# A gated delta rule in chunks of 64 on 64x64 TensorE tiles, its blocks inverted on VectorE, in front of a Fourier mixing block

## The chip, the core and the metric

The kernel runs on one core of a Trainium2 chip. TensorE multiplies matrices, VectorE, ScalarE and GpSimd work on elements, SyncE (SP) issues most transfers. The metric is the device time of one execution in microseconds; lower is better.

## What is computed

Four batches, eight heads, 768 tokens of 48 channels. Per head a 48x48 state is read by the query and corrected by each token; the heads' outputs, side by side (384 channels), go through a Fourier mixing over tokens and channels, a normalization and a two-layer channel mix.

```python
for t in range(S):
    y[:, :, t] = np.einsum('bhd,bhde->bhe', q[:, :, t], state)
    v_old = np.einsum('bhde,bhd->bhe', state, kt)
    state = state + bt[:, :, :, None] * np.einsum('bhd,bhe->bhde', kt, vt - v_old)
...
X = np.fft.fft(np.fft.fft(x, axis=1), axis=2)
u = x + np.real(X)
un = (u - mu) / np.sqrt(var + 1e-06)
out = u + np.maximum(un @ w_ch1, 0.0) @ w_ch2
```

All matrix work is in float32; the two weights arrive as 64-bit floats and are turned into float32 on VectorE, with a last multiplication on GpSimd.

## The kernel before, in words

The attention goes through each batch in six chunks of 128 tokens, 24 chunks in all, each with all eight heads. `load` fetches K, V and q of a chunk. `pre(n)` normalizes K (a power on GpSimd, L304), transposes keys and queries on TensorE (`pt`, L321), forms the Gram products (`pg`, L337) and from them `AT`, `LQ` and the block-diagonal `Abd`. Within a chunk, tokens depend on earlier ones through a triangular matrix. `pre` inverts its 32x32 diagonal blocks in five levels (loop at L361): `px` multiplies a widened block-diagonal matrix by the inverse so far, VectorE masks it into `Y`, `widen` (L353) spreads `Y` and the transposed inverse over 128 columns on VectorE and GpSimd, and `pn` multiplies again. Each of these matmuls has a 128x128 weight and 32 moving columns, one for each head.

`seq(n)` is the chain over chunks: `pk` (keys times state, L410), `R`, then four times over a 32-row strip `pu` (L425), a copy `U` on ScalarE, `pa` (L420) and a subtraction; then `pS` (the state's update, L433), `py` (the output, L437 and L439), and the state's add on VectorE (L443).

`post(b)` does all that follows for a batch: sums and differences on VectorE and the matmuls `pf`, `pb`, `pd` of the Fourier stage, their adds into `x` (L512), statistics, and in three groups of 256 tokens the transposes `ptr`, the first layer `ph` (L566, 36 matmuls of 256 columns), relu on ScalarE and VectorE in turn, the second layer `po` (L577, 24 matmuls of 384 columns), and the stores.

`weights()` converts the six 1.5 MB pieces of the two weights. All of these are generators. The loop at L599 takes a piece of `seq(n)`, a piece of `pre(n + 1)` and a piece of `side` in turn; `side` is `weights()` during batch 0 and `post(b - 1)` after. `post` of the last batch stands alone behind the loop. The framework's scheduler then fixes each engine's order from these pieces; every engine works in order. A float32 matmul shows as two records in the trace, a weight load (PEld) and a matmul (PE) for each.

Of the kernel before, what the change touches and what calls it, by code (L numbers as in the profile page):

```python
# [16 lines left out]
C = 128  # L17
W = 32
LEVELS = (1, 2, 4, 8, 16)


def _consts(B, S, DM):

    p = np.arange(128)
    c = np.arange(W)
    r = p % W
    ident = np.eye(128)
    su = (p[None, :] > p[:, None]).astype(np.float64)
    bd = su * (p[None, :] // W == p[:, None] // W)
    grp = (p[:, None] // W == np.arange(128 // W)[None, :]).astype(np.float64)  # L30
    eye_c = (r[:, None] == c[None, :]).astype(np.float64)
    lev = []
    for n in LEVELS:
        off = ((r[:, None] // n) % 2 == 1) & (c[None, :] // n == r[:, None] // n - 1)
        lev.append(eye_c - off)
    pack = np.concatenate([ident, su, bd, grp, eye_c] + lev, axis=1)
# [45 lines left out]
def kernel(  # L82
# [23 lines left out]
    HV = (5 * H + 7) // 8  # L106
# [4 lines left out]
    io = ctx.enter_context(tc.tile_pool(name="io", bufs=2))  # L111
# [3 lines left out]
    def ps_pre(shape, name):  # L115
        return ps.tile(shape, F32, tag="pre", bufs=3, name=name)

    def ps_seq(shape, name):
        return ps.tile(shape, F32, tag="seq", bufs=2, name=name)

    def ps_post(shape, name):
        return ps.tile(shape, F32, tag="post", bufs=3, name=name)
# [9 lines left out]
    NKQ = 2  # L132
    kqs = []
    for i in range(NKQ):
        t = const.tile([128, 3, H, 64], F32, name=f"kq{i}")
        nc.gpsimd.memset(t, 0.0)
        kqs.append(t)
    states = []
    for i in range(2):
        t = const.tile([128, NP, 2, D], F32, name=f"state{i}")  # L140
        nc.gpsimd.memset(t, 0.0)
        states.append(t)

    steps = [(b, c) for b in range(B) for c in range(NC)]
    loaded = {}

    def load(n):
        b, c = steps[n]
        kq = kqs[n % NKQ]
        K4 = io.tile([128, H, D], F32, tag="K4", name="K4")  # L150
        V4 = io.tile([128, H, D], F32, tag="V4", name="V4")

        first = c * C + (1 if c < TH else 0)
        m = C - 1 if c == TH - 1 else C
        cuts = (0, 112, m) if m < C else (0, m)
        for dst, src in ((K4, k), (kq[:, 2, :, 0:D], q), (V4, v)):
            for i, j in zip(cuts, cuts[1:]):
                nc.sync.dma_start(out=dst[i:j],
                                  in_=src[b, :, first + i:first + j, :].rearrange("h p d -> p h d"))
            if m < C and src is q:  # L160
                nc.sync.dma_start(out=dst[m:C],
                                  in_=cn["zrow"].ap().rearrange("p (h d) -> p h d", h=H))
            elif m < C:
                nc.sync.dma_start(out=dst[m:C],
                                  in_=src[b, :, 0:1, :].rearrange("h p d -> p h d"))
        loaded[n] = (K4, V4)

    pack = const.tile([128, 3 * 128 + NG + W * (1 + len(LEVELS))], F32, name="pack")
    nc.scalar.dma_start(out=pack, in_=cn["pack"].ap())
    bt = const.tile([NBH, S], F32, name="bt")  # L170
    bflat = beta.rearrange("b h s -> (b h) s")
    nc.gpsimd.memset(bt[:, S // 2 - 1:S // 2], 0.0)
    nc.scalar.dma_start(out=bt[:, 0:S // 2 - 1], in_=bflat[:, 1:S // 2])
    nc.scalar.dma_start(out=bt[:, S // 2:S], in_=bflat[:, S // 2:S])
    load(0)
# [10 lines left out]
    m_su = pack[:, 128:256]  # L186
    m_bd = pack[:, 256:384]
    o = 3 * 128
    m_grp = pack[:, o:o + NG]
    eye_c = pack[:, o + NG:o + NG + W]  # L190
    m_lev = [pack[:, o + NG + W * (i + 1):o + NG + W * (i + 2)] for i in range(len(LEVELS))]

# [455 lines left out]
```

## Time and profile before

| | |
|---|---|
| median of 3 runs | 1946.74 us (1942.17 to 1961.88) |
| profiled execution | 1932.67 us |
| its span, first to last instruction | 1930.9 us |
| TensorE matmuls busy | 1843.2 us, 95% |
| TensorE weight loads busy | 1626.1 us, 84% |
| VectorE busy | 629.6 us, 33% |
| GpSimd busy | 449.5 us, 23% |
| ScalarE busy | 244.1 us, 13% |
| mean granted clock of TensorE | 0.895 |

How to read it: busy time is the time in which an engine has an instruction in work, so 95% says that something is nearly always in TensorE, not that its array is full. [...] Durations of single matmul records overlap, since they are pipelined; what a group costs is read from the time that it takes as a whole.

### The profile page before, as it was taken

How to read it: one execution, taken by the hardware profiler on the slowest of the kernel's cores; microseconds unless marked ns; L12 is line 12 of the kernel's file. 1: busy time of each engine (PE TensorE's matmuls, PEld its weight loads, DVE VectorE, ACT ScalarE, POOL GpSimd, SP SyncE). 2: the span in 40 equal slices, each digit the busy share in tenths (PEclk: the TensorE clock that was granted, in tenths of full speed). 3: DMA queues.
4: the chain of work that ended last, by engine and by line, in shares of the span. 5: the costliest groups of instructions: out<-in, count | busy, mean ns of one | idle time of the engine just before them, and what ended most of it. 6: DMA issues, size and time to landing. Idle time of an engine off the chain costs nothing. (4 is left out here: it accounts for less than half of the span.)

```text
span 1930.9 us, 26464 instructions
## 1 busy us (share of the span) xinstructions
PE 1843.2 (95%) x11782; PEld 1626.1 (84%) x11782; DVE 629.6 (33%) x1142; ACT 244.1 (13%) x481; POOL 449.5 (23%) x381
## 2 busy tenths in 40 slices
PE   5899898989999999999999999999999999999898
PEld 5898898989898897988888987888798888888576
DVE  4333433433323321323242332323323333222410
ACT  0101011010111101111101011101110111111110
POOL 3331312222221221313220322233211232122100
PEclk9999999999999857879975599999955699899899
DMA  5101101000000000001000000000000000000000
GB/s 145 38 9 41 37 5 45 9 5 13 5 5 5 13 9 9 13 13 21 9 13 5 9 14 18 9 14 21 13 9 1 13 9 9 1 9 2 9 8 17
DMA packets 80710, 31.47 MB, mean 16 GB/s; under 512 B 76116, under 2 KB 77716, under 8 KB 80212
## 3 DMA queue, kind: packets, MB, share of 16 engines
q1 hardware_dynamic: 78964, 25.96, 5.7%
q0 software_dynamic: 768, 2.36, 0.3%
q8 instruction: 92, 1.51, 0.3%
q10 hardware_dynamic: 864, 1.47, 0.2%
q14 instruction: 22, 0.18, 0.0%
HBM read 25.06 MB, written 4.72 MB: 15 GB/s over the span
## 5 line engine op out<-in xcount | busy, mean ns | idle before, releaser
L125 PEld LDWEIGHTS pn<-Tn,Yx 128*128 128x128 f32 x1536 | 259.9, 260 | 23.9 <-issue 18.1
L125 PE MATMUL pn<-Tn,Yx 128*128 128x32 f32 x1536 | 255.5, 331 | 16.5 <-DVE Yx L356 15.2
L125 PE MATMUL ph<-unT,w 128*128 128x256 f32 x864 | 248.8, 431 | 1.9 <-ACT unT L560 1.9
L356 POOL TENSOR_TENSOR TTx<-Tn,pack 128x384 f32<-128x384 f32 x96 | 133.6, 1392 | 482.0 <-ACT Tn L385 385.9
L356 POOL TENSOR_TENSOR Yx<-Y,pack 128x384 f32<-128x384 f32 x120 | 146.3, 1220 | 392.7 <-DVE Y L368 321.3
L125 PEld LDWEIGHTS px<-Tn,Abd 128*128 128x128 f32 x1152 | 197.0, 264 | 29.1 <-ACT Tn L385 25.2
L125 PE MATMUL px<-Tn,Abd 128*128 128x32 f32 x1152 | 200.0, 339 | 16.8 <-ACT Tn L385 16.8
L125 PEld LDWEIGHTS pn<-Y,TTx 128*128 128x128 f32 x1152 | 196.2, 262 | 19.2 <-DVE Y L368 15.2
L125 PE MATMUL po<-w,hT 128*128 128x384 f32 x576 | 209.9, 503 | 0.0
L125 PE MATMUL pn<-Y,TTx 128*128 128x32 f32 x1152 | 195.8, 335 | 10.8 <-DVE Y L368 10.8
L356 DVE TENSOR_TENSOR TTx<-Tn,pack 128x640 f32<-128x640 f32 x96 | 83.4, 869 | 374.5 <-ACT Tn L385 313.6
L125 PEld LDWEIGHTS ph<-unT,w 128*128 128x128 f32 x864 | 172.0, 213 | 27.8 <-ACT unT L560 2.8
L125 PEld LDWEIGHTS po<-w,hT 128*128 128x128 f32 x576 | 104.6, 193 | 56.6 <-issue 0.6
L125 PE MATMUL pg<-KQT,K1T 48*128 48x128 f32 x768 | 143.6, 369 | 2.7 <-ACT KQT L323 2.7
L125 PEld LDWEIGHTS pg<-KQT,K1T 48*128 48x128 f32 x768 | 117.7, 254 | 15.7 <-ACT KQT L323 4.4
L368 DVE TENSOR_TENSOR Y<-px,pack 128x256 f32<-128x256 f32 x120 | 50.8, 424 | 242.1 <-PE px L125 242.1
L356 DVE TENSOR_TENSOR Yx<-Y,pack 128x640 f32<-128x640 f32 x120 | 126.5, 1054 | 5.7 <-DVE Y L368 0.5
L125 PEld LDWEIGHTS pu<-R,Tn 32*32 32x32 f32 x1536 | 94.3, 130 | 33.1 <-issue 16.3
L385 ACT ACTIVATE Tn<-pn 128x512 f32<-128x512 f32 x72 | 43.0, 597 | 593.6 <-PE pn L125 569.0
L421 DVE TENSOR_TENSOR R<-R,pa 32x384 f32<-32x384 f32 x72 | 39.8, 553 | 218.1 <-PE pa L125 217.9
L125 PE MATMUL pu<-R,Tn 32*32 32x48 f32 x1536 | 109.6, 236 | 0.7
L125 PEld LDWEIGHTS pa<-U,AT 64*32 64x32 f32 (+2 forms) x1152 | 71.9, 134 | 21.0 <-issue 15.0
(107 smaller groups left out, 1826.3 us busy)
## 6 DMA issues: line engine op xcount, KB each, us to landing
w<-in_moe_w_ch_dram SPq DMA_DIRECT2D x6, 1536.0 KB
K<-in_k_dram SPq DMA_DIRECT2D x20, 192.0 KB
V<-in_v_dram SPq DMA_DIRECT2D x20, 192.0 KB
kq<-in_q_dram SPq DMA_DIRECT2D x20, 192.0 KB
out_dram<-x SPq DMA_DIRECT2D x8, 192.0 KB
kq<-in_q_dram SPq DMA_DIRECT2D x4, 168.0 KB
K<-in_k_dram SPq DMA_DIRECT2D x4, 168.0 KB
V<-in_v_dram SPq DMA_DIRECT2D x4, 168.0 KB
```

The lines of the kernel that those rows point to most:

```text
L125: nc.tensor.matmul(o, lhsT=lhsT, rhs=rhs, start=start, stop=stop, skip_group_check=True)
L356: eng.tensor_tensor(t[:, hs], src[:, hs, None, :].broadcast_to(shape), m_grp[:, None, :, None].broadcast_to(shape), op=ALU.mult)
L368: nc.vector.tensor_tensor(Y, px, m_lev[i][:, None, :].broadcast_to([128, H, W]), op=ALU.mult)
L385: nc.scalar.activation(Tn, pn, ACT.Copy)
L421: nc.vector.tensor_tensor(R[rw], R[rw], pa[rw], op=ALU.subtract)
```

## The change

The attention is written anew; `post`, `weights` and the stores keep their arithmetic.

- Chunks have 64 tokens, 48 in all. Four heads lie side by side in the lower half of the partitions and four in the upper half (`hh`), and four chunks make a quad, of which there are 12. A quad's K, q and V come in 24 loads.
- `prepare(Q)` does for a quad what `pre` did up to the Gram products. `pg` is a matmul of 48 rows by 64 columns; the four combinations of row half (`e`) and column half (`hh`) follow each other.
- `invert(g)` takes two quads: eight chunks of eight heads with two blocks of 32x32 each, 128 blocks, one for each partition. Four 32x32 block transposes on VectorE bring each block onto one partition (`X`, 32x32 elements), 30 steps of a multiplication and an addition with broadcasts invert all of them, and six transposes bring them back. Four rounds of 32 small matmuls (`pj`, 32x32x32) join the two blocks of a chunk, and GpSimd scales the result `wt` by beta.
- `chain(m)` has no strips: `pk`, `R`, one `pu`, `U`, `pS` with the state's add (two state tiles in turn), `py`.
- The loop takes six pieces of `pre` (now `prepare` and `invert` of the group ahead) and eight of `side` for each chunk. The first group is prepared and inverted wholly before the first chunk.
- In PSUM, buffers are two pairs of banks, two single ones and two for `post` (three before). The weight staging and `hT` have one buffer (two before), K and q one.

```diff
-C = 128
+CH = 64
...
+    def invert(g):
+        A = grams.pop(g)
+        wt = wts[g % 2]
+        X = wk.tile([128, W, W], F32, tag="X", name="X")
+        for i in range(4):
+            pr, c0 = slice(32 * i, 32 * i + 32), W * (i % 2)
+            nc.vector.transpose(X[pr], A[pr, :, :, c0:c0 + W].rearrange("p c u s -> p s (c u)"))
+        yield
+        for j in range(1, W - 1):
+            n = W - 1 - j
+            t = wk.tile([128, 240], F32, tag="sub", bufs=2, name="sub")
+            t = t[:, 0:n * j].rearrange("p (k i) -> p k i", k=j)
+            nc.vector.tensor_tensor(t, X[:, j:j + 1, j + 1:].broadcast_to([128, j, n]),
+                                    X[:, 0:j, j:j + 1].broadcast_to([128, j, n]), op=ALU.mult)
+            nc.vector.tensor_tensor(X[:, 0:j, j + 1:], X[:, 0:j, j + 1:], t, op=ALU.add)
+            if j % 2 == 0:
+                yield
...
+        for lh in range(2):
+            js = wk.tile([128, QT, 4, W], F32, tag="js", name="js")
+            for step in range(2):
...
+                            if step == 0:
+                                ops = A[r2, n, u, 0:W], wt[r2, n, u, W:]
+                            else:
+                                ops = T1[r1, n, u], js[r1, c, u]
+                            mm(pj[r1, hh, c, u], *ops, c == 0 and u == 0)
...
+            nc.gpsimd.tensor_tensor(w, w, bb[:, :, :, None].broadcast_to([128, QT, 4, CH]), op=ALU.mult)
...
-        for j in range(NP):
-            mm(pk[:, 2 * j:2 * j + 2, :], KQT[:, 0, j, :], st[:, j], j == 0)
+        for j in range(2):
+            for hh, e in ((0, 0), (1, 1), (0, 1), (1, 0)):
+                pr = slice(64 * e, 64 * e + D)
+                mm(pk[64 * hh:64 * hh + 64, e, j], KQT[pr, c, j, hh, 0, :], st[pr, hh, j, e, :], j == 0)
...
-        for g in range(NG):
...
-                for h in range(H):
-                    mm(pa[rw, h, :], AT[0:W * g, h, rw], U[0:W * g, h, :], h == 0)
...
+        for u in range(4):
+            for hh in range(2):
+                pr = slice(64 * hh, 64 * hh + 64)
+                mm(pu[pr, u], wt[pr, at, u], R[pr, u], u == 0)
...
+    run(ahead(0))
+    tables()
+    side, pre = weights(), iter(())
+    for m in range(STEPS):
...
+        live = True
+        step = chain(m)
+        shares = [6, 8]
+        while live or any(shares):
+            live = live and advance(step)
+            for i, gen in enumerate((pre, side)):
+                for _ in range(2):
+                    if shares[i]:
+                        shares[i] -= 1
+                        advance(gen)
+    run(side)
+    run(post(B - 1))
```

TensorE before, at a chunk of batch 2 that runs beside the first layer of `post(1)` (`ident` and `eye` start each level's product, `x3` means three in a row):

```order
L125 MATMUL ph<-unT,w_98 128x256 x2
L125 LDWEIGHTS ident_b
L125 MATMUL px<-eye_b,ident_b 128x256
L125 MATMUL px<-Y,Abd 128x32 x8
L125 MATMUL ph<-unT,w_98 128x256 x3
L125 MATMUL pn<-Y,TTx 128x32 x8
L125 MATMUL ph<-unT,w_98 128x256 x3
L125 MATMUL pn<-Tn,Yx 128x32 x8
```

TensorE in the change, a chunk of batch 1 beside the first layer of `post(0)`:

```order
L124 MATMUL pk<-st_76,KQT 64x48 x8
L127 MATMUL ptr<-pack,un 128x128 x6
L124 MATMUL pu<-R,wt_74 64x48 x8
L124 MATMUL ph<-unT,w_125 128x256 x18
L124 MATMUL pS<-U,kp_64 48x48 x8
L124 MATMUL py<-st_76,KQT 64x96 x4
L124 MATMUL py<-U,LQ 64x48 x8
L124 MATMUL ph<-unT,w_125 128x256 x12
```

Where the inverse's matmuls stood between pieces of `ph`, the chain's own groups of eight stand now, and a whole chunk passes within some thirty `ph`.

VectorE in the change, between the last chunk of batch 1 and the first of batch 2: the end of `invert` (`X`, `wt`, `T`) and of the Fourier stage of `post(1)` (`x<-x,pb`), then `R` of the chunk:

```order
L377 TENSOR_TENSOR sub<-X 128x30
L554 TENSOR_TENSOR x<-x,pb 128x193
L379 TENSOR_TENSOR X<-X,sub 128x30
L585 BN_AGGR mv<-bst 128x2
L554 TENSOR_TENSOR x<-x,pb 128x191
L386 STREAM_TRANSPOSE wt_74<-X 32x32x32
L389 STREAM_TRANSPOSE T_3656<-X 32x32x32
...
L597 TENSOR_SCALAR un<-x,mv,rstd 128x384 x3
L452 TENSOR_TENSOR R<-V_3247,pk 128x2x2x48
```

TensorE at the same place:

```order
L124 MATMUL pb<-dtab,F 128x191 x2
L124 MATMUL pd<-dtab,gz 32x193 x2
L124 MATMUL pj<-wt_74,A 32x32 x32
L124 MATMUL pj<-js,T_3656 32x32 x32
L124 MATMUL pj<-wt_74,A 32x32 x32
L127 MATMUL ptr<-pack,un 128x128 x6
L124 MATMUL pj<-js,T_3656 32x32 x32
L124 MATMUL pk<-st_76,KQT 64x48 x8
```

Here the inverse of the next group, the whole Fourier stage and the four rounds of `pj` stand in front of the first chunk of the batch on both engines.

## Rows read from the trace of the kernel before

**Rows 1.** Page: busy times, granted clock in 40 slices, transfer rate by slice.
```profile
PE 1843.2 (95%) x11782; PEld 1626.1 (84%) x11782; DVE 629.6 (33%) x1142; ACT 244.1 (13%) x481; POOL 449.5 (23%) x381
...
PEclk9999999999999857879975599999955699899899
...
GB/s 145 38 9 41 37 5 45 9 5 13 5 5 5 13 9 9 13 13 21 9 13 5 9 14 18 9 14 21 13 9 1 13 9 9 1 9 2 9 8 17
```

**Rows 2.** Groups of TensorE by form: busy us, mean ns; idle before, releaser.
```profile
L125 PE MATMUL pn<-Tn,Yx 128*128 128x32 f32 x1536 | 255.5, 331 | 16.5 <-DVE Yx L356 15.2 <-DVE nrm L306 1.2
L125 PE MATMUL ph<-unT,w 128*128 128x256 f32 x864 | 248.8, 431 | 1.9 <-ACT unT L560 1.9
L125 PE MATMUL po<-w,hT 128*128 128x384 f32 x576 | 209.9, 503 | 0.0
L125 PE MATMUL px<-Tn,Abd 128*128 128x32 f32 x1152 | 200.0, 339 | 16.8 <-ACT Tn L385 16.8
L125 PE MATMUL pn<-Y,TTx 128*128 128x32 f32 x1152 | 195.8, 335 | 10.8 <-DVE Y L368 10.8
```

**Rows 3.** Timeline, 100 to 118 us: start, duration, engine, instructions, idle before.
```profile
103.51 3.46 PE L125 MATMUL px<-pack,Abd 128*128 128x32 f32 x16
106.90 1.48 PE L125 MATMUL pu<-R,Tn 32*32 32x48 f32 x16
...
108.42 0.48 ACT L426 ACTIVATE U<-pu 32x384 f32<-32x384 f32 x1 [7.61 <-PE pu L125]
...
108.95 1.09 PE L125 MATMUL pS<-U,kq 128*64 128x48 f32 x16 [0.57 <-ACT U L426]
```

**Rows 4.** Timeline, two places at the higher clock, 1152 and 1195 us.
```profile
1152.14 1.03 PE L125 MATMUL pk<-state,KQT 128*128 128x96 f32 x8
...
1153.00 1.91 PE L125 MATMUL px<-Tn,Abd 128*128 128x32 f32 x16
...
1195.66 2.85 PE L125 MATMUL po<-w,hT 128*128 128x384 f32 x8
...
1198.44 0.67 PE L125 MATMUL pS<-U,kq 128*64 128x48 f32 x16
```

**Rows 5.** By stage: length, busy of PE, PEld, DVE, ACT, POOL; clock; DMA.
```profile
640.00:1114.00 474.00, 469.01 (x3046) 411.50 (x3044) 147.13 (x271) 61.84 (x122) 115.37 (x100) 0.75 0.05 12
1114.00:1404.00 290.00, 289.44 (x2343) 246.25 (x2342) 96.48 (x165) 47.18 (x95) 79.91 (x64) 0.98 0.07 15
1404.00:1527.00 123.00, 119.69 (x608) 111.08 (x607) 40.91 (x88) 13.47 (x25) 25.13 (x26) 0.50 0.04 7
...
1800.00:1931.00 131.00, 115.33 (x472) 84.19 (x471) 31.50 (x86) 13.59 (x31) 8.81 (x12) 0.96 0.03 11
```

**Rows 6.** Timeline, the first load of K and its first use.
```profile
0.72 0.45 SPq L158 DMA_DIRECT2D K<-in_k_dram  x1
...
4.59 0.82 POOL L301 TENSOR_TENSOR Ksq<-K 128x384 f32<-128x384 f32 x1
```

**Rows 7.** Groups of VectorE by form.
```profile
L339 DVE TENSOR_TENSOR Abd<-pg,pack 128x512 f32<-128x512 f32 x48 | 33.2, 691 | 66.2 <-PE pg L125 66.1
...
L512 DVE TENSOR_TENSOR x<-x,pb 128x191 f32<-128x191 f32 x72 | 20.9, 346 | 0.0
...
L412 DVE TENSOR_TENSOR R<-Vb,pk 128x384 f32<-128x384 f32 x24 | 13.1, 545 | 11.4 <-PE pk L125 11.4
...
L267 DVE TENSOR_SCALAR wtmp<-w 128x768 int32<-128x768 int32 x12 | 7.2, 601 | 6.7 <-POOL w L286 6.6
```

**Rows 8.** Groups of ScalarE and GpSimd by form.
```profile
L382 ACT ACTIVATE Tn<-pn 128x256 f32<-128x256 f32 x48 | 18.4, 384 | 262.5 <-PE pn L125 246.2 <-DVE wtmp L271 9.8 <-POOL nrm L304 6.6
...
L304 POOL TENSOR_TENSOR nrm<-nrm,half_p 128x8 f32<-128x8 f32 x24 | 41.6, 1732 | 22.6 <-DVE nrm L303 22.6
...
L286 POOL TENSOR_TENSOR w<-wtmp 128x768 f32<-128x768 f32 x12 | 24.0, 2000 | 30.4 <-DVE wtmp L285 28.8 <-DVE nrm L305 1.6
...
L546 POOL TENSOR_TENSOR rstd<-rstd,half_n 128x2 f32<-128x2 f32 x12 | 8.7, 728 | 1.0
```

More of the change, by code (lines that the diff above doesn't have):

```diff
@@ L15 @@
 ACT = mybir.ActivationFunctionType
-C = 128
+CH = 64
 W = 32
-LEVELS = (1, 2, 4, 8, 16)
+QT = 4
 def _consts(B, S, DM):
     p = np.arange(128)
[L25 to L36, printed above, removed]
+    t = np.arange(CH)
+    before = (t[None, :] > p[:, None] % CH).astype(np.float64)
+    lower = -(t[None, :] < p[:, None] % CH).astype(np.float64)
+    pack = np.concatenate([np.eye(128), before, lower], axis=1)
     half = S // 2
@@ L129, in tr @@
                          is_transpose=True, start=start, stop=True, skip_group_check=True)
[L132 to L144, printed above, removed]
-    loaded = {}
@@ L147, in load @@
[L147 to L166, printed above, removed]
@@ L168, with zeroed @@
-    pack = const.tile([128, 3 * 128 + NG + W * (1 + len(LEVELS))], F32, name="pack")
+    def zeroed(shape, name, eng):
+        t = const.tile(shape, F32, name=name)
+        eng.memset(t, 0.0)
+        return t
+    kps = [zeroed([128, QT, 4, 64], f"kp{i}", nc.gpsimd if i else nc.vector) for i in range(NB)]
+    qps = [zeroed([128, QT, 4, 64], f"qp{i}", nc.vector) for i in range(1)]
+    wts = [zeroed([128, 2 * QT, 4, CH], f"wt{i}", nc.gpsimd) for i in range(2)]
+    sts = [zeroed([128, 2, 2, 2, D], f"st{i}", nc.gpsimd) for i in range(2)]
@@ L352, in widen @@
-        def widen(src, tag):
-            t = wk.tile([128, H, NG, W], F32, tag=tag, name=tag)
-            for eng, hs in ((nc.vector, slice(0, HV)), (nc.gpsimd, slice(HV, H))):
-                shape = [128, hs.stop - hs.start, NG, W]
-                eng.tensor_tensor(t[:, hs], src[:, hs, None, :].broadcast_to(shape),
-                                  m_grp[:, None, :, None].broadcast_to(shape), op=ALU.mult)
-            return t.rearrange("p h g w -> p h (g w)")
-        T = TT = TTx = None
@@ L444, in seq @@
-        nc.scalar.activation(xs[b][:, c if c < TH else NC + TH - 1 - c, :], py.rearrange("p h d -> p (h d)"), ACT.Copy)
+        last = n == NCH - 1
+        pk = ps_pair("pk")[:, :, 0:2 * D].rearrange("p e (j d) -> p e j d", j=2)
+        for j in range(2):
+            for hh, e in ((0, 0), (1, 1), (0, 1), (1, 0)):
+                pr = slice(64 * e, 64 * e + D)
+                mm(pk[64 * hh:64 * hh + 64, e, j], KQT[pr, c, j, hh, 0, :], st[pr, hh, j, e, :], j == 0)
+        R = wk.tile([128, 4, D], F32, tag="R", bufs=2, name="R")
@@ new lines, in chain @@
+        if not last:
+            pS = ps_pair("pS")[:, :, 0:2 * D].rearrange("p h (j d) -> p h j d", j=2)
+            for j in range(2):
+                for hh, e in ((0, 0), (1, 1), (0, 1), (1, 0)):
+                    pr = slice(64 * hh, 64 * hh + 64)
+                    mm(pS[64 * e:64 * e + D, hh, j], kp[pr, c, 2 * j + e, 0:D], U[pr, 2 * j + e], j == 0)
+            for e in range(2):
+                pr = slice(64 * e, 64 * e + D)
+                nc.vector.tensor_tensor(nst[pr, :, :, e, :], st[pr, :, :, e, :], pS[pr], op=ALU.add)
```

396 lines of the change are left out of this document (212 added, 184 removed).

## The prediction

> **What bounds the kernel now.** I read the page's busy times first. TensorE's matmuls fill 95% of the span, VectorE, GpSimd and ScalarE a third or less [rows 1]: this is a TensorE kernel. Then the groups of its instructions, shapes apart: three groups of the triangle inverse (`pn`, `px`; 128-column weights, 32 moving columns) take 651 us, the two products of the channel mix (`ph`, `po`) 459 us [rows 2]. Third, the clock. [...] In the rows by stage the granted clock is 0.50 in 1404 to 1527, where TensorE is as busy as elsewhere, but with short attention matmuls and the Fourier stage, 0.98 in 1114 to 1404, where `ph` and `po` run beside them, and 0.96 at the end, where the post stage runs alone [rows 5]. So attention is not only the larger half of the work, it also holds the clock down where nothing else runs.
>
> **What goes, what comes.** The inverse by levels goes: `pn`, `px` (the 651 us and their smaller groups), the widening `Yx`, `TTx` on VectorE and GpSimd, and the serial `pu`, `pa` ladder of 32-row strips. The post stage stays instruction for instruction. What comes, by prices:
>
> *TensorE.* Attention now works in 64x64 tiles. The nearest row is `pS`, already 64 columns wide and on two column halves in turn: sixteen records (eight matmuls) in 0.67 us at full clock [rows 4], 1.09 at half [rows 3]. I take that for each of `pk`, `pu`, `pS` and the `LQ` part of `py`. Below it: half, if four tiles run at once. Above it: 1.91, the 128-column price [rows 4]. The state part of `py` (four matmuls, 96 columns) I put at 0.6, between half of `pk`'s 1.03 [rows 4] and all of it. One chunk: 4 x 0.67 + 0.6 = 3.3 us. Per eight chunks `prepare` and `invert` add 32 transposes (0.12 each from 1.91 / 16, 3.8 us), 64 `pg` matmuls of 128 columns in two tiles (0.12, 7.7) and 128 `pj` matmuls of 32 columns (0.06, 7.7): 2.4 per chunk. Changing tile shape costs about 0.1: `px` starts 0.17 before the modelled end of `pk`, same shape, `pS` 0.07 before that of `po` [rows 4]. Eight changes a chunk: 0.8. Together 6.5 us per chunk, 48 chunks, 312 us, where attention now takes some 1,300 of 1843 (`ph`, `po` and the small Fourier groups taken off).
>
> *The chain.* A chunk is `pk`, `R` on VectorE, `pu`, `U` on ScalarE, `pS`, and `py` before the next `pk`; the state's add (0.35 twice) lies beside `py`. With TensorE otherwise empty, so at the lower clock: 3 x 1.09 + 0.35 + 0.38 + (1.09 + 1.3) + about 0.4 of hand-offs (0.05 from `U`'s end at 108.90 to `pS` [rows 3]) = 6.8 us. 192 elements on VectorE cost 0.35 [rows 7].
>
> *VectorE.* Two rows give a price, 0.346 for 191 elements and 0.545 for 384 [rows 7]: 0.15 us and 1.03 ns an element. `invert`'s sixty multiply and add instructions hold 9,920 elements in all: 9 + 10.2 = 19 us per eight chunks. No row shows STREAM_TRANSPOSE. Ten of them with 1,024 elements: by the same price 1.2 each, which I take, 12 us (floor 0.35 each, 4; ceiling double, 24). Two `prepare` add 10.8 (reduction and scaling of 768 elements 0.94 each, `A` and `LQ` 0.69 each four times [rows 7], small ones 0.6). Together 42 us per eight chunks. GpSimd's power on 16 columns: 0.73 for 2, 1.73 for 8 [rows 8], so 3.1.
>
> *Costed at nothing.* ScalarE's new copies (48 `U` at 0.38, 48 `x`, 48 to 72 transposed chunks, 48 `pj`, by 0.38 for 256 elements [rows 8]) and GpSimd's masks stay under a third of the span and run beside TensorE. SP now issues 24 loads a quad in place of 6 for the same tokens; at 0.45 [rows 6] that is 11 us in the 60 and more that a quad will take. The q loads wait for the last chunk transposes of the quad before, K's for its scaling, and a weight piece and the next V wait behind them in SP's queue. Their cover is the rest of the quad; without it a quad's `prepare` starts some 11 us late, 12 times, and half of that, 65 us, is in the range.
>
> **The sum by stages, along the new order.**
> 1. *Before the first `pu`* nothing hides the set-up. K comes in eight issues of 0.45 instead of one that let the square start at 4.59 [rows 6]: 7.7; square 2, reduction 0.9, power 3.1, rest 1.7: 15.4. Chunk transposes and Gram products at half clock: 28. Second quad: 46. Then the inverse: transposes 5, the sixty 19, thirty weight instructions between them 14 (0.45; 0.60 for 768 elements [rows 7]), transposes out 7: 91. The four `pj` rounds are serial (matmuls 1.9, two copies 0.6 each, hand-offs): 14; GpSimd's scaling of `wt`, twice 1,024 elements at 2.0 per 768 [rows 8]: 5. **110 us.**
> 2. *Batch 0, twelve chunks.* VectorE sets it: weights, 11 parts of ten instructions, 50; `pre` of the next group 42, half of the one after 11; chain 13; the second `pj` and scaling, 19; and seven chunks with little on VectorE, where the chain is 3 us longer each: 22. **157 us.** The single weight buffer adds a load behind each piece; the order puts transposes and small rows ahead of the next use, about 10 us. At the 145 GB/s of the page's first slice [rows 1] a load of 1.57 MB is 11 us, so uncovered loads would cost up to 5 x 11 = 55: that goes into the range.
> 3. *Batches 1 to 3.* Post alone now takes 126 of the last 131 us with TensorE busy 115 [rows 5]. To its 126 add the attention's 12 x 6.5 = 78; the inverse's tail of 19 us one and a half times a batch, half of it beside `ph`, 14; three chunks after post has run out, 10; the Fourier stage at the lower clock, 10; less the 16 us that TensorE idles in the window, which attention fills. 222 each, **666 us.** Relu copies lie behind at most eight small rows (2.5 us) on VectorE; two `ph` matmul groups in front of them cover 2.6.
> 4. *Post of batch 3*, as now: **131 us.**
>
> 110 + 157 + 666 + 131 = 1064. The profiled execution is 1932.67 for a span of 1930.9, and the median of the runs stands 0.7% above it: (1064 + 2) x 1.007 = **1075 us.**
>
> **Rivals.** (a) *Post does not keep the clock up.* A matmul burst is now followed by chain waits. [...] For it: 0.75 over 640 to 1114, although TensorE was never idle there [rows 5]. Against: `ph` and `po` will be over half of TensorE's time, more than in the stretch at 0.98. Chance 0.12. [...]
> (b) *Tiles take turns.* If 64x64 tiles in different rows don't overlap as the column halves of `pS` do, a group of eight costs 1.1 in place of 0.67 (16 records at half the 128-column spacing, and the tail): about 3.4 more per chunk on 36 chunks, 35 in the first stages: 1230 us. Chance 0.1.
> (c) *Small VectorE rows are dear.* `invert`'s pairs depend on each other; at 0.67 instead of 0.32 each, 360 rows add 126, and they stand ahead of `R`: 1200 us. Chance 0.1.
> (d) *Better than priced.* Four tiles at once, transposes at their floor, loads all covered: 36 x 2 + 50 less, some 950. Chance 0.12.
> (e) *Slower than before.* The same place as (c): 870 us over 360 rows needs 2.4 us more for each, seven times the nearest row. Chance 0.02.
> My forecast keeps 0.54 with 990 to 1170 as its own range.
>
> **Range and chances.** From below (d)'s middle to most of (a): 960 to 1300. Faster by over 1% 0.97, within 1% (about what a measurement of this kernel can tell from no change) 0.01, slower 0.02; every case but (e) ends far below.
>
> **What would show it.** The first `pu` near 110 us; twelve `py` of batch 0 done by about 270; `pk` of batch 2 after a gap of some 50 us, behind `X` rows and Fourier rows on VectorE; groups of eight 64-column matmuls at 0.67 us; the clock at 1.0 under `ph` and `po` and 0.5 in set-up and batch 0; post alone at the end for 131 us. TensorE busy should fall from 95% to some 65%. Wrong would be a first `pu` after 150, `pS` over 1 us at full clock, a low clock under `ph`, or STREAM_TRANSPOSE over 2.4 us.

## The result, and the profile after

The changed kernel takes 1004.83 us (median of 4 runs, 999.34 to 1005.39); the kernel before took 1944.61 us on the same chip. The ratio is 0.515 (95% interval 0.512 to 0.518). The forecast was 1075, with a range of 960 to 1300. The profiled execution is 1004.53 us, its span 1002.8.

First the page: the busy row of TensorE with the others, and the granted clock in forty slices. Columns of the busy row: us, share of the span, instructions.

```profile
PE 748.7 (75%) x7768; PEld 566.9 (57%) x7768; DVE 547.6 (55%) x1200; ACT 150.5 (15%) x337; POOL 172.4 (17%) x136
...
PEclk9555556555586989997557999999879999879999
```

TensorE's 95% of [rows 1] is 75% of half the time, and VectorE's share went from a third to 55%. The clock digits stand at 5 to 6 until a quarter of the span is over, and at 7 to 9 for nearly all of the rest; the two 5s in the middle are the gap ahead of batch 2 (below). The 9 of the first slice is not what the rows there show: two `pt` records take 0.63 us at 19.11, as they do at 478.62, in that gap, where the granted clock is 0.50.

The span in the stages of the prediction: set-up (to the first `pk`), batch 0 (to the end of its last `py`), batches 1 to 3 with the post stage of the batch before, the last post. Columns: stretch, length, busy time of TensorE matmuls, weight loads, VectorE, ScalarE and GpSimd (instructions), granted clock, DMA share, GB/s.

```profile
0.00:118.00 118.00, 29.70 (x480) 23.83 (x480) 78.33 (x155) 11.02 (x21) 43.33 (x33) 0.62 0.30 70
118.00:267.40 149.40, 82.87 (x1342) 70.66 (x1341) 119.74 (x253) 21.41 (x47) 40.54 (x26) 0.53 0.23 61
267.40:478.20 210.80, 179.60 (x1805) 134.27 (x1804) 113.64 (x248) 34.91 (x80) 34.20 (x26) 0.86 0.12 24
478.20:692.30 214.10, 184.55 (x2060) 137.24 (x2060) 122.89 (x268) 39.34 (x88) 34.86 (x27) 0.87 0.11 23
692.30:870.20 177.90, 159.34 (x1640) 118.01 (x1638) 81.64 (x195) 29.99 (x70) 11.95 (x13) 0.94 0.05 12
870.20:1002.80 132.60, 112.62 (x456) 82.87 (x454) 31.37 (x85) 13.79 (x31) 7.52 (x11) 0.93 0.03 9
```

| stage | forecast | measured |
|---|---|---|
| up to the first `pu` | 110 | 121.0 (the first `pk` stands at 118) |
| batch 0, to its last `py` | 157 | 146.4 |
| batches 1 to 3, to the last `py` | 666 | 602.8 |
| post of batch 3 | 131 | 132.6 |
| sum | 1064 | 1002.8 |

Set-up and batch 0 miss by 11 us each, in opposite directions; the last post is met. What is left of the difference is in batches 1 to 3, which are 63 us shorter than forecast.

The timeline of TensorE in batch 3, where a chunk runs between pieces of `ph` (columns: start, time that the group took, engine, line, operation, tiles, records):

```profile
744.94 0.40 PE L124 MATMUL pS<-U,kp 64*48 64x48 f32 x16
745.26 0.87 PE L124 MATMUL py<-st,KQT 128*64 128x96 f32 x8
...
746.07 0.67 PE L124 MATMUL py<-U,LQ 64*64 64x48 f32 x16
746.67 5.45 PE L124 MATMUL ph<-unT,w 128*128 128x256 f32 x24
752.04 0.45 PE L124 MATMUL pk<-st,KQT 48*64 48x48 f32 x16
752.42 2.86 PE L124 MATMUL ph<-unT,w 128*128 128x256 f32 x12
...
755.21 0.67 PE L124 MATMUL pu<-R,wt 64*64 64x48 f32 x16
```

`pS` and `pk`, which go round four tiles, take 0.40 and 0.45 here, with a granted clock of 1.00; `pu` and the `LQ` part, which have two tiles, take the 0.67 that the prediction put on all four. The state part of `py` takes 0.87, where 0.6 was forecast.

What attention cost TensorE in batches 1 to 3 is told by the whole of that stretch for one tile name each, in the order `pg`, `pj`, `pt`, `pk`, `pu`, `pS`, `py` (columns: busy time of matmuls, of weight loads, of the engine that reads the result, clock):

```profile
267.40:870.20 602.80, 19.29 (x448) 14.77 (x448) 18.03 (x28) 0.89 0.10 20
267.40:870.20 602.80, 22.71 (x1024) 20.48 (x1024) 18.80 (x32) 0.89 0.10 20
267.40:870.20 602.80, 20.14 (x112) 14.13 (x112) 17.17 (x44) 0.89 0.10 20
267.40:870.20 602.80, 20.65 (x576) 15.32 (x576) 12.53 (x36) 0.89 0.10 20
267.40:870.20 602.80, 26.65 (x576) 22.54 (x576) 11.95 (x36) 0.89 0.10 20
267.40:870.20 602.80, 13.60 (x528) 9.31 (x528) 23.20 (x66) 0.89 0.10 20
267.40:870.20 602.80, 56.04 (x866) 46.47 (x864) 17.50 (x36) 0.89 0.10 20
```

Together 179.1 us for 36 chunks, 5.0 a chunk. `pk`, `pu`, `pS` and `py`, the chain, are 3.25 of them; `pg`, `pj` and `pt`, the preparation, 1.73.

The set-up: rows of its timeline at the places that the prediction named (SPq is SP issuing transfers; in brackets the engine's idle time before, and what ended it).

```profile
0.72 5.81 SPq L160 DMA_DIRECT2D K<-in_k_dram  x8
...
10.72 1.47 POOL L307 TENSOR_TENSOR Ksq<-K 128x768 f32<-128x768 f32 x1 [0.28 <-DMA K<-in_k_dram]
...
31.39 1.47 POOL L307 TENSOR_TENSOR Ksq<-K 128x768 f32<-128x768 f32 x1 [6.93 <-DMA qp<-in_q_dram]
...
49.47 7.58 DVE L371 STREAM_TRANSPOSE X<-A 32x1024 f32<-32x1024 f32 x4
...
106.15 1.91 DVE L386 STREAM_TRANSPOSE wt<-X 32x1024 f32<-32x1024 f32 x1
...
117.94 0.68 PE L124 MATMUL pk<-st,KQT 48*64 48x48 f32 x16
...
121.05 1.04 PE L124 MATMUL pu<-R,wt 64*64 64x48 f32 x16
```

The first quad's square waits for K until 10.72, the second's until 31.39: SP works through K, q and V of the first quad, and K has one buffer. (SP's issues of the second quad's K end at 29.4; the row names q, whose issues follow them.)

The block transposes over the whole execution, by line (busy us, mean ns of one):

```profile
L386 DVE STREAM_TRANSPOSE wt<-X 32x1024 f32<-32x1024 f32 x24 | 46.3, 1930 | 0.6
L371 DVE STREAM_TRANSPOSE X<-A 32x1024 f32<-32x1024 f32 x24 | 45.7, 1902 | 0.2
```

And the gap ahead of batch 2, from `R` of chunk 23 at 473.95 to `pk` of chunk 24 at 532.63: VectorE's groups in 474.3 to 533.2.

```profile
L379 DVE TENSOR_TENSOR X<-X,sub 128x168 f32<-128x168 f32 (+14 forms) x24 | 9.4, 390 | 0.1
L377 DVE TENSOR_TENSOR sub<-X 128x184 f32<-128x184 f32 (+14 forms) x23 | 9.3, 404 | 0.1
L554 DVE TENSOR_TENSOR x<-x,pb 128x191 f32<-128x191 f32 (+1 forms) x24 | 7.9, 349 | 1.7 <-PE pb L124 1.6
L386 DVE STREAM_TRANSPOSE wt<-X 32x1024 f32<-32x1024 f32 x4 | 7.6, 1899 | 0.1
```

VectorE is busy for 47.7 of these 58.9 us; inverse rows (`X`, `sub`, transposes) and Fourier rows (`x`) follow each other, and the chain's next chunk needs the last of the inverse. The same kind of gap (58 us, with weight conversions in place of Fourier rows) stands between chunks 7 and 8, in batch 0.

### The profile page after: what moved, and what is told of

Its sections match the earlier page's. It is cut to its first block, busy times and chain, and to the rows that moved or that the text cites. A ratio compares the mean times of both kernels' runs of the same rounds, so it can differ in the third digit from the quotient of the medians.

```text
span 1002.8 us, 18113 instructions
## 1 busy us (share of the span) xinstructions
PE 748.7 (75%) x7768; PEld 566.9 (57%) x7768; DVE 547.6 (55%) x1200; ACT 150.5 (15%) x337; POOL 172.4 (17%) x136
## 4 chain that ended last, share of the span: by engine, by line
PE 51%; DVE 30%; POOL 5%; SPq 5%; issue 4%; DMA 2%; ACT 2%; POOLq 0%; DVEq 0%; ACTq 0%
PE ph L124 17%; PE po L124 14%; PE py L124 5%; DVE X L371 5%; SPq L160 4%; DVE sub L377 3%; DVE X L379 3%; DVE wt L386 3%; DVE x L554 3%; PE pf L124 3%; PE pu L124 3%; PE pj L124 2%; PE pg L124 2%; POOL nrm L310 2%; DVE T L389 2%
## 5 line engine op out<-in xcount | busy, mean ns | idle before, releaser
L124 PE MATMUL ph<-unT,w 128*128 128x256 f32 x864 | 208.3, 396 | 5.8 <-DVE hT L613 4.0
L613 DVE TENSOR_SCALAR hT<-ph 128x256 f32<-128x256 f32 x72 | 30.4, 422 | 119.7 <-PE ph L124 119.4
L379 DVE TENSOR_TENSOR X<-X,sub 128x30 f32<-128x30 f32 (+9 forms) x180 | 62.7, 348 | 3.3
L377 DVE TENSOR_TENSOR sub<-X 128x30 f32<-128x30 f32 (+9 forms) x180 | 61.6, 342 | 2.9
L124 PE MATMUL py<-st,KQT 128*64 128x96 f32 x384 | 50.4, 284 | 5.7 <-DVE LQ L357 5.7
L124 PE MATMUL pu<-R,wt 64*64 64x48 f32 x768 | 39.1, 251 | 14.8 <-DVE R L452 14.8
L124 PEld LDWEIGHTS pu<-R,wt 64*64 64x64 f32 x768 | 33.8, 164 | 26.7 <-POOL wt L415 9.2
L472 DVE TENSOR_TENSOR st<-st,pS 48x192 f32<-48x192 f32 x88 | 30.9, 351 | 31.9 <-PE pS L124 30.3
L386 DVE STREAM_TRANSPOSE wt<-X 32x1024 f32<-32x1024 f32 x24 | 46.3, 1930 | 0.6
L371 DVE STREAM_TRANSPOSE X<-A 32x1024 f32<-32x1024 f32 x24 | 45.7, 1902 | 0.2
L124 PEld LDWEIGHTS py<-st,KQT 128*64 128x64 f32 x384 | 40.0, 159 | 10.2 <-issue 4.3
```

The lines of the kernel that those rows point to most:

```text
L124: nc.tensor.matmul(o, lhsT=lhsT, rhs=rhs, start=start, stop=stop, skip_group_check=True)
L371: nc.vector.transpose(X[pr], A[pr, :, :, c0:c0 + W].rearrange("p c u s -> p s (c u)"))
L377: nc.vector.tensor_tensor(t, X[:, j:j + 1, j + 1:].broadcast_to([128, j, n]), X[:, 0:j, j:j + 1].broadcast_to([128, j, n]), op=ALU.mult)
L379: nc.vector.tensor_tensor(X[:, 0:j, j + 1:], X[:, 0:j, j + 1:], t, op=ALU.add)
L386: nc.vector.transpose(wt[pr, :, :, c0:c0 + W].rearrange("p c u t -> p t (c u)"), X[pr].rearrange("p s t -> p t s"))
L472: nc.vector.tensor_tensor(nst[pr, :, :, e, :], st[pr, :, :, e, :], pS[pr], op=ALU.add)
```

## The experiments

All of them start from the changed kernel. The table gives, from each trace, the start of `R` (the subtraction on VectorE, once a chunk) for the first chunk of each batch and the last of all, the end of the span, and the median time.

| kernel | chunk 0 | 12 | 24 | 36 | 47 | span | median us |
|---|---|---|---|---|---|---|---|
| changed kernel | 119.7 | 272.6 | 533.4 | 694.3 | 867.7 | 1002.8 | 1004.83 |
| e1_turn | 125.2 | 292.6 | 567.3 | 746.5 | 930.5 | 1066.7 | 1070.82 |
| e3_postapart | 119.8 | 403.7 | 674.7 | 919.0 | 1021.7 | 1159.4 | 1160.15 |
| e2_noconv | 117.8 | 239.6 | 497.1 | 663.5 | 838.9 | 979.3 | 978.10 |
| e8_fill | 119.4 | 265.3 | 530.1 | 695.6 | 872.7 | 1009.0 | 1010.45 |
| e7_norows | 85.9 | 219.3 | 467.6 | 658.7 | 847.3 | 984.5 | 989.04 |
| e5_nb4 | 121.3 | 281.7 | 505.8 | 703.9 | 887.1 | 1028.7 | 1028.89 |
| e6_start | 122.6 | 265.0 | 529.0 | 697.0 | 871.3 | 1011.1 | 1013.45 |
| e6b_vlate | 103.2 | 255.6 | 521.9 | 688.1 | 863.5 | 1003.9 | 1003.75 |
| e4_pack | 107.0 | 246.4 | 485.1 | 645.5 | 818.5 | 956.5 | 953.54 |
| c1_packv | 93.8 | 243.8 | 482.1 | 643.0 | 814.5 | 950.9 | 951.88 |
| c2_all | 95.3 | 251.0 | 471.0 | 665.0 | 838.6 | 978.6 | 979.98 |
| c3_shares | 92.3 | 220.6 | 442.8 | 616.8 | 779.2 | 925.4 | 927.60 |

**Do the tiles work at once?** Rival (b) against the forecast. In five groups the loops over tiles and over heads change places; `pk` as an example:

```diff
-        for j in range(2):
-            for hh, e in ((0, 0), (1, 1), (0, 1), (1, 0)):
+        for hh, e in ((0, 0), (1, 1), (0, 1), (1, 0)):
+            for j in range(2):
                 pr = slice(64 * e, 64 * e + D)
```

> One order is changed: in pk, pu, pS, the LQ part of py and pg all matmuls of one 64x64 tile follow each other, where the changed kernel goes to another tile each time. Theory (tiles work at once): with neighbours on one tile the groups of eight lengthen, at full clock pk from 0.45 towards 0.8, pS from 0.40 towards 0.75, pu and LQ from 0.67 to about 1.0, pg from 1.05 towards 1.6; some 1.8 us more per chunk on TensorE, 36 chunks at full clock 65 us, of which the waits around hide half: 1025 to 1070. Rival (a group is short because its matmuls are small, whatever tile they use): groups unchanged within 0.05 us, time within 5 us of 1005.

Measured: 1070.82 us, 66 more. The same stretch (batches 1 to 3), for `pg`, `pu` and `py`; compare with 19.29, 26.65 and 56.04 above.

```profile
287.70:930.50 642.80, 45.99 (x448) 40.66 (x448) 18.05 (x28) 0.87 0.09 19
287.70:930.50 642.80, 37.70 (x560) 33.12 (x560) 11.55 (x35) 0.87 0.09 19
287.70:930.50 642.80, 67.30 (x842) 57.75 (x843) 17.45 (x36) 0.87 0.09 19
```

Where four matmuls now follow each other on one tile, the group takes 2.4 times as long (`pg`) or 1.4 times (`pu`; 0.94 instead of 0.67 at full clock). Where only two do, next to nothing is lost: `pk` 0.47, `pS` 0.41. That part of the expectation was wrong; the time came out 0.8 above its upper end. So the time of `pg`, `pu` and the `LQ` part hangs on the tiles of their neighbours: tiles do work together. Whether one tile multiplies while another multiplies or while another loads its weights, these rows don't part, and that `pk` and `pS` are shorter than `pu` because they have four tiles and not two is argued, not shown.

**What the post stage gives the attention.** Its pieces are taken from between the chunks and run at the end of the batch.

```diff
-            side = post(b - 1)
+            run(post(b - 1))
+            side = iter(())
```

> The post stage of batches 0 to 2 no longer runs beside the next batch's attention: all of it is emitted at the batch's end, ahead of the next batch's first chunk. Theory (post covers the chain's waits and the gap behind the inverse, and keeps the clock up): 118 and 165 as they are, then three times 131 for post and some 130 to 150 for attention at the lower clock with nothing beside it, and 131: 1200 to 1260. Rival (the gap of 58 us is VectorE's and the chain costs little): attention alone 90 per batch: about 1080; if the attention can be prepared during post, less.

Measured: 1160.15 us. The rows by stage, post of batch 0, attention of batch 1, and so on in turn:

```profile
267.40:403.00 135.60, 118.70 (x462) 87.58 (x462) 39.47 (x100) 13.68 (x31) 13.20 (x13) 0.87 0.05 13
403.00:520.00 117.00, 62.06 (x1307) 52.30 (x1306) 73.59 (x143) 20.98 (x48) 19.74 (x13) 0.66 0.14 27
520.00:674.20 154.20, 128.52 (x761) 96.02 (x759) 59.15 (x147) 18.57 (x40) 17.89 (x14) 0.84 0.05 12
674.20:783.00 108.80, 59.11 (x1302) 50.08 (x1302) 63.06 (x126) 20.97 (x48) 19.85 (x13) 0.70 0.15 29
783.00:918.50 135.50, 121.13 (x507) 89.60 (x506) 32.55 (x89) 14.06 (x32) 6.85 (x10) 0.90 0.04 11
918.50:1022.00 103.50, 58.33 (x1144) 49.76 (x1144) 52.93 (x110) 16.18 (x38) 4.75 (x3) 0.59 0.03 7
```

The six stretches are 754.6 us, where the interleaved kernel has 602.8: side by side is worth 152 us. Attention alone runs at a granted clock of 0.59 to 0.70 and leaves TensorE idle for nearly half of its time; interleaved, the clock is 0.86 to 0.94. The theory's mechanism stands, its size not (the total is 40 us under its range): attention alone takes 104 to 117, not 130 to 150. A second reason is in the third row: part of the next inverse lies in the post stage, which is 154 there.

**What sets batch 0.** Two kernels ask the same from both sides. In the first, nine of the ten VectorE instructions that convert a part of the weights are left out.

```diff
-                nc.vector.tensor_scalar(man, man, 0x3F800000, None, op0=ALU.bitwise_or)
...
-                nc.vector.tensor_tensor(exp, exp, low, op=ALU.bitwise_or)
```

> Nine of the ten VectorE instructions that turn a part of the weights into float32 are left out (18 parts; the weights are then not the reference's). About 80 us of VectorE leave the first 283 us. Theory (VectorE sets batch 0): batch 0 from 165 to 105 to 125 us, first pk some 8 earlier (two parts stand between the steps of the first inverse), total 945 to 965. Rival (the chain at the lower clock sets it): batch 0 still 150 or more, total 985 to 1000.

Measured: 978.10 us. Set-up and batch 0:

```profile
0.00:117.00 117.00, 29.14 (x476) 23.33 (x476) 66.70 (x117) 10.91 (x21) 42.92 (x38) 0.61 0.37 98
117.00:237.70 120.70, 67.91 (x1346) 58.07 (x1342) 67.86 (x137) 21.28 (x47) 30.02 (x22) 0.67 0.21 50
```

In the second, matmuls that nobody reads keep TensorE busy.

```diff
+    def filler():
+        pz = ps_post([128, 256], "pz")
+        for _ in range(2):
+            mm(pz, ident, stab[:, 0:256], True)
```

> Two matmuls of 128x128 by 256 columns, whose result nobody reads, are added at each of the 90 steps of the weights' conversion, to keep TensorE busy in batch 0. Theory (VectorE sets batch 0): the granted clock there goes from 0.54 to 0.8 or more, the chain's groups get shorter, yet batch 0 stays at 158 to 170 us; total 1000 to 1012. Rival (the chain at the lower clock sets it): batch 0 falls by 20 or more, total 985 or less.

Measured: 1010.45 us, in the same stretches as the changed kernel's first two rows:

```profile
0.00:118.00 118.00, 91.86 (x782) 76.10 (x782) 77.19 (x156) 11.87 (x23) 43.65 (x33) 0.91 0.29 70
118.00:267.40 149.40, 90.91 (x1469) 72.81 (x1470) 121.24 (x257) 22.22 (x51) 39.09 (x26) 0.69 0.24 64
```

Most of the filler landed in the set-up, whose clock rose from 0.62 to 0.91 without moving the first `R` (119.4 against 119.7). In batch 0 the clock rose from 0.53 to 0.69, not to the 0.8 that was expected, and batch 0 (chunk 0 to chunk 12 in the table) took 146 instead of 153. Without the conversions it took 122, with a clock of 0.67 there. So of its 31 us some 7 may be the clock's and the rest is VectorE's work, the larger part, as forecast; what batch 0 would take at full clock throughout was not measured. But VectorE is not all: with its busy time down to 56% of the stretch, the gap between chunks 7 and 8 is still 47 us, and the expected total was missed by 13 us, since the set-up gained 2 instead of 8 and 9 of the 33 us gained by chunk 12 were lost again by the end.

**What the inverse costs.** The sixty small instructions of the inverse are left out, so that blocks are transposed and not inverted.

```diff
-            nc.vector.tensor_tensor(t, X[:, j:j + 1, j + 1:].broadcast_to([128, j, n]),
-                                    X[:, 0:j, j:j + 1].broadcast_to([128, j, n]), op=ALU.mult)
-            nc.vector.tensor_tensor(X[:, 0:j, j + 1:], X[:, 0:j, j + 1:], t, op=ALU.add)
```

> The sixty small multiplications and additions of the inverse are left out (the blocks are transposed, not inverted). VectorE does 120 us less in all, 20 in each of six groups. Theory (the inverse stands on the path in the set-up and in the gaps of 58 us): first pk at 95 to 100, both gaps 35 to 42 us, total 920 to 950. Rival (the rows lie beside GpSimd, the conversions and post; the gaps are the transposes', the joining rounds' and the buffers'): only the set-up gains, total 975 to 990.

Measured: 989.04 us, the rival's case. The first chunk starts 34 us earlier, and by the end 18 are left. The gaps do not vanish, they move: one of 40 us between chunks 5 and 6, one of 57 between chunks 13 and 14. In the second, the state's add of chunk 13 starts at 283.46, behind conversions, Fourier rows, transposes and `x` rows, in VectorE's fixed order. Taking 120 us of work from VectorE moved the end by 16: behind the set-up, the order in which its rows stand seems to decide more than their sum. (The last run below, with the same work in another order, is 24 us faster than its base.)

**Are the buffers the cause of the gaps?** With three buffers, the second quad of the next group can be prepared only when the group's fifth chunk begins.

```diff
-    NB = 3
+    NB = 4
...
-        wt = wts[g % 2]
+        wt = wts[g] = A
...
+                    if step == 0:
+                        nc.gpsimd.memset(A[64 * hh + W:64 * hh + 64, QT * lh:QT * lh + QT, :, 0:W], 0.0)
```

> Four buffers instead of three for keys, transposed keys and masked Gram products of a quad; to make room, the inverse is written into the tile of the Gram products (two of these, and a clearing of 32 columns on GpSimd), and small tiles share a tag. Theory (the gaps of 58 us ahead of the ninth chunk of batches 0 and 2 stand there because the second quad of the next group can be prepared only when the group's fifth chunk begins): both gaps shrink to 20 or less; in batch 2 most of this is gained (30 to 40), in batch 0 VectorE's conversions take part of it (10 to 20); total 950 to 970. Rival (VectorE's and GpSimd's work per group fills the time anyway): the gaps move, total 990 to 1010.

Measured: 1028.89 us, slower than with three. The gap ahead of chunk 24 is gone (6 us), but batch 2 then takes 198 us where it took 161, so that from chunk 12 to chunk 36 both kernels need 422 us. In batch 0 the gap moved from chunks 7 and 8 to chunks 5 and 6 (51 us). The theory falls: an earlier inverse takes the same time from another chunk. The rival was right in kind; 1029 lies beyond its range. The time lost lies in the set-up and batch 0 (9 us), batch 3 (10) and behind the last chunk (7); what costs it there no run tells. That its way back writes to another tile also cost a little (transposes of 2.18 us in place of 1.93), which is not parted from the rest here.

**The set-up.** First, q and V of two quads on ScalarE's queue, and a second buffer for K:

```diff
+            eng = nc.scalar if Q < 2 and src is not k else nc.sync
...
-        K4 = wk.tile([128, QT, 4, D], F32, tag="K4", name="K4")
+        K4 = wk.tile([128, QT, 4, D], F32, tag="K4", bufs=2, name="K4")
```

> The q and V loads of the first two quads are issued by ScalarE instead of SP, and K has a second buffer, so that the second quad's K is asked for right behind the first's. Theory (SP's 0.6 us per issue and the one K buffer delay the second quad: its square starts at 31.39 though GpSimd was idle from 24.5): the square starts at about 18 to 20, all of the set-up behind it 11 to 13 earlier, first pk at 105 to 108, total 990 to 995. Rival (what follows, the weight conversions between the inverse's steps, or ScalarE's own issues ahead of its copies, takes it up): first pk at 115 to 120, total 1000 to 1008.

Measured: 1013.45 us. The second square starts at 16.63, as the theory has it, but the first `pk` at 120.9: ScalarE's issues stand ahead of its copies of `KQT` (issues from 24.4, the next copy at 29.5), the weights' first load goes out earlier (14.4 instead of 55), and their conversions and the next group's preparation slip in ahead of the inverse, whose first transpose starts at 51.3 (49.5 before). The rival was right in kind; the total lies 5 us beyond its range, and where these are lost no run tells. Second, with all loads on SP, and only the order changed:

```diff
-    values(0)
+    early[1] = wk.tile([128, QT, 4, D], F32, tag="unT", bufs=2, name="K4")
+    fetch(1, (early[1], k))
...
     run(ahead(0))
+    values(0)
```

> The second quad's K is asked for behind the first quad's q, into a buffer of its own, and the V loads only behind the second quad's q; all on SP. Theory: the second quad's square starts at 18 to 21 instead of 31.39, first pk at 105 to 110, total 990 to 997. Rival (as in the run with ScalarE's issues, other work of VectorE slips in ahead of the inverse): first pk 115 or later, total 1000 to 1010.

Measured: 1003.75 us, which is no change: the set-up is the theory's (2.5 us better at the first `pk`), the total the rival's. The rows at the two places:

```profile
23.53 1.47 POOL L309 TENSOR_TENSOR Ksq<-K 128x768 f32<-128x768 f32 x1 [6.56 <-DMA K<-in_k_dram]
...
102.47 0.68 PE L124 MATMUL pk<-st,KQT 48*64 48x48 f32 x16
```

The set-up shrinks by 15 us and none of it arrives. The table shows where it goes: 17 ahead at chunk 12, 12 at chunk 24, 6 at chunk 36, 4 at the last. What fits this, though no run parts it: the weights' first load starts at 54 as before (55), and their last part is converted at 264 (271 before), so the rows in front of batch 1 end only 7 us earlier.

**Three transposes instead of ten.** ScalarE packs the diagonal blocks of all 128 partitions side by side, one transpose brings them in, two bring them back, and ScalarE spreads the result.

```diff
-            nc.vector.transpose(X[pr], A[pr, :, :, c0:c0 + W].rearrange("p c u s -> p s (c u)"))
+            nc.scalar.activation(Dg[pr], A[pr, :, :, c0:c0 + W], ACT.Copy)
+        nc.vector.transpose(X, Dg.rearrange("p c u s -> p s (c u)"))
...
+        nc.vector.transpose(Dw.rearrange("p c u t -> p t (c u)"), X.rearrange("p s t -> p t s"))
+        nc.vector.transpose(T1.rearrange("p c u s -> p s (c u)"), X)
+            nc.scalar.activation(wt[pr, :, :, c0:c0 + W], Dw[pr], ACT.Copy)
```

> The ten block transposes of a group (four in, six out, each on 32 partitions, 1.9 us each) become three on 128 partitions; ScalarE packs the diagonal blocks ahead (four copies) and spreads the result behind (four copies). Theory (a transpose costs by its columns, whatever its partitions): 1.9 us each again, 13.3 us of VectorE less per group; before the first pk 13.3 less 2 to 4 for the copies, so some 108; the gaps of 58 us ahead of batch 0's and batch 2's ninth chunk shrink by 8 to 13; total 955 to 985. Rival 1 (cost by elements): transposes of 4 to 7.6 us, total 1005 or more. Rival 2 (the gaps are set by the buffers and GpSimd, not by VectorE): only the set-up gains, 993 to 997.

Measured: 953.54 us, 51 less (ratio to the kernel before 0.490, 0.486 to 0.494). The transposes by line:

```profile
L387 DVE STREAM_TRANSPOSE Dw<-X 128x1024 f32<-128x1024 f32 x6 | 12.3, 2055 | 0.2
L373 DVE STREAM_TRANSPOSE X<-Dg 128x1024 f32<-128x1024 f32 x6 | 11.6, 1936 | 4.3 <-ACT Dg L372 4.3
L388 DVE STREAM_TRANSPOSE T<-X 128x1024 f32<-128x1024 f32 x6 | 11.5, 1923 | 0.0
```

128 partitions take about the 1.9 us of 32, so the instruction is not paid by its partitions. (Every one here has 1,024 columns, so no row parts a price per column from a fixed one.) The gain came as the theory had it in size (1.5 us beyond its range), but not in place: 13 in the set-up, 13 in batch 0 and 22 in batch 1, while the gaps ahead of chunks 8 and 24 kept 56 and 58 us. These rows show the four groups of 32 partitions done in the time of one; what they take, with whatever is fixed in it, is 1.9 ns a column (1,024 in 1.9 us), nearly twice the 1.03 ns that two other rows give beside a fixed 0.15 us [rows 7].

**Together.** The packed transposes with the earlier K:

> Two edits together: the three transposes on 128 partitions (alone 953.54) and the earlier second K with V behind it (alone 1003.75, first pk at 102.5 but the gain given back later). Theory (the two gains in the set-up add and what follows is VectorE's work, now lower): first pk at 88 to 94, total 938 to 948. Rival (what the set-up gains is given back behind it, as it was alone): first pk at 88 to 94, total 950 to 957.

Measured: 951.88 us, within the noise of the packed kernel alone: the set-up's gain is lost again, now within batch 0 (107.0 to 93.8 at chunk 0, 246.4 to 243.8 at chunk 12). Then four buffers and five pieces of preparation a chunk on top:

> The two edits of the run before, the four buffers (alone 1028.89) and 5 instead of 6 pieces of preparation per chunk. Theory (four buffers cost time only because VectorE had no room for an earlier inverse; with 13 us less per group and the pieces spread it has): no gap over 25 us at the ninth chunk of batches 0 and 2, total 915 to 938. Rival (an earlier inverse is put ahead of the chain's R and state rows on VectorE, whatever the room): total 955 to 985.

Measured: 979.98 us, 28 more than without. The gap ahead of chunk 24 is 7 us, and batch 2 again pays for it (194 against 161). More room on VectorE does not save the four buffers. Last, on the kernel with the two edits, the rate at which post is handed out:

```diff
-        shares = [6, 8]
+        shares = [6, 6]
```

> As the run with the two edits, and 6 instead of 8 pieces of post per chunk, so that its 70 pieces last for all twelve chunks of the next batch and not for nine. Theory (the last three chunks of a batch have nothing beside them and run at the lower clock): these chunks run beside ph and po at full clock, 10 to 25 less than the run with the two edits. Rival (post only ends later, the chain's waits stay): within 5 of that run.

Measured: 927.60 us (926.23 to 928.90), 24 less than with 8, and the fastest of all: 0.476 of the kernel before (0.474 to 0.479), 77 us under the changed kernel. Its rows from the end of chunk 12 to the end of the chain, cut at the first chunk of batches 2 and 3:

```profile
228.50:442.00 213.50, 180.71 (x1960) 133.50 (x1953) 128.92 (x311) 53.74 (x97) 45.56 (x33) 0.87 0.13 30
442.00:616.00 174.00, 167.63 (x1812) 123.02 (x1809) 78.39 (x199) 43.59 (x88) 26.88 (x22) 0.97 0.12 26
616.00:780.00 164.00, 150.60 (x1549) 110.48 (x1548) 66.28 (x185) 36.86 (x74) 11.06 (x12) 0.94 0.03 8
```

With 8 pieces a chunk the last `po` of batch 0 ends at 412.6, ahead of chunks 22 (418.4), 23 (424.9) and the gap of 57 us behind them. With 6 it ends at 424.5, and chunk 23 (413.7) and part of the inverse lie beside it: the gap ahead of chunk 24 is 29 us. But the table puts 23 of the 24 us ahead of any post, in batch 0, where side work is the conversion: with fewer of its rows between the chunks, chunk 12 starts 23 us earlier (220.6 against 243.8), and the last part is converted at 256 instead of 243, in batch 1. From chunk 12 to the end the two kernels need 705 and 707 us: batches 1 and 3 are 16 and 9 us shorter, batch 2 13 and the end behind the last chunk 10 longer. So the theory's place for the gain is not borne out. Since 17 us gained by chunk 12 were lost again in e6b_vlate, it is not refuted either: no run changes the rate beside the conversions or beside post alone.

## Why the prediction came out

**Set-up, 110 forecast, 121 measured.** Sound, with three terms too small and one too large. The block transposes were put at 1.2 us and take 1.9: 18.8 for ten instead of 12. The steps of the inverse with what stands between them took from 57.46 to 96.87, 39 instead of 33, since rows of the next quad's preparation stand among them too. SP's issues take 0.73 each in the first eight, not 0.45, and the first square starts at 10.72, not at 7.7. From the last transpose's end to the first `pu`, joining and scaling, it is 13 us instead of 19. At the lower clock (0.50 granted from 121 to 123 us) `pu` takes the 1.04 to 1.09 that was priced from [rows 3]. That [rows 3] stand at half clock was the author's estimate from their times (sixteen `px` records take 3.46 us there and 1.91 in [rows 4]); the granted clock in that trace is 1.00 at both places.

**Batch 0, 157 forecast, 146 measured.** "Twelve `py` of batch 0 done by about 270" was met, at 267.4, by luck: set-up and batch 0 miss by 11 us in opposite directions. "VectorE sets it" is borne out by the runs without conversions (31 us less) and with a higher clock (7 us less), with the limit named there: a gap of 47 us is left even with VectorE half idle. VectorE is busy for 119.7 of the 149.4 us from the first `pk`, where the forecast's terms for it (50, 42, 11, 13) add up to 116; what was too large is the rest, 41, of which 30 came.

**Batches 1 to 3, 666 forecast, 603 measured.** This is the step that was mis-sized, in one term. The sum had, over three batches, 234 of attention on TensorE, 345 of post and 87 idle (29 a batch: 11 in post alone, 14, 10 and 10, less 16). Measured: attention 179.1, the rest of TensorE's 523.5 busy us, 344.4, and 602.8 less 523.5, 79.3, idle. So 55 of the 63 us are the price of a chunk: 5.0 and not 6.5. Its parts show where. The four groups of the chain had the right sum, 3.25 a chunk where 3.28 was forecast, by luck in part: at full clock `pk` and `pS` are together 0.5 cheaper and the state part of `py` is 0.27 dearer, and the lower clock of some stretches (0.89 granted over all three batches) may take up the rest, which no run parts. What did not come is the 0.8 for eight changes of shape: from the start of `pS` (744.94) to the next `ph` (746.67) three groups of different shapes pass in 1.73 us, less than their 1.94 added up. That is 29 of the 55 us. Nearly all of the rest, 24, are `prepare` and `invert`, 2.4 a chunk in the forecast and 1.73 here: by an estimate at the prices measured, some 14 of them are work that had been done beside batch 0 (`pg` has 448 records in this stretch, nine quads' worth would be 576) and that the forecast charged to all 36 chunks; 10 are lower prices.

**From the span to the median** the forecast added 11 us (two, then 0.7%, as in the kernel before); here it was 2.

**Last post, 131 forecast, 132.6 measured**, as in [rows 5].

**The gap.** "`pk` of batch 2 after a gap of some 50 us, behind `X` rows and Fourier rows on VectorE" is what the rows of 474 to 533 show, with 58.

**The rivals.** (a) falls: the clock is 0.86 to 0.94 beside post, and the run with post apart shows that post is what holds it up (0.59 to 0.70 without). No run shows the time near 1300 that the range takes from it; with post wholly apart the kernel takes 1160. (b) falls by the run that makes tiles take turns; even that costs 66 us, not the 155 that the rival put on it. (c) falls: the small rows take 0.19 to 0.52 us by form, 0.35 on average, against 0.32 forecast. (d) came in part: its 2 us a chunk came nearly (1.5), but for another reason than four tiles at once, and the transposes are dearer, not cheaper. (e) fell with (c).

**What the forecast missed.** TensorE is busy 75% of the span, not some 65%; the 65 had no sum behind it, and 113 of the 749 us lie in set-up and batch 0 at little more than half clock (0.62 and 0.53 granted). And the forecast took time in the set-up and batch 0 as additive. It is not: 15 us saved there alone gave nothing at the end, and 34 gave 16.

## What to carry to other kernels

Issue the matmuls of small TensorE tiles so that neighbours use different tiles (66 us here), and charge nothing for a change of shape that no row shows (29 us of forecast here). Where a stage's preparation is done beside the stage before, charge it there. When an engine works in a fixed order, time taken out in front can be lost at the next place where a chain's row stands behind a block of other work (15 and 34 us of set-up came to 0 and 16 here): test a gain alone before it is added to a sum. And try the rate at which side work is handed out: here that one number was worth 24 us, nearly half of what the set-up and transpose edits brought together (53), though it is not shown beside which side stage.

## What was unexpected of the hardware

A block transpose of 1,024 columns takes 1.9 us on 32 partitions and 1.9 to 2.1 on 128, some 1.9 ns a column, where two other float32 rows of VectorE give 1.03 beside a fixed 0.15 us [rows 7].

Four float32 matmuls in a row on one 64x64 tile cost (`pg` 45.99 us against 19.29 for the same chunks), two in a row hardly do (`pk` 0.47 against 0.45).

A granted clock of 0.91 instead of 0.62 in the set-up changed the start of the first `R` by 0.3 us.
